# Lightning attention into a locality-gated expert layer: weights asked for behind the rows of x, routing's products sooner, first pair's preparation ahead of its gates, triples' turning later

## The chip, the cores and the metric

The kernel runs on one core of a Trainium2 chip. The metric is the device time of one execution, in microseconds (us). Before the change the median of three runs is 476.42 us (474.8 to 478.07).

The engines are named as in the profile: PE multiplies matrices (PEld is its weight load), DVE is the vector engine, ACT the scalar engine, POOL issues the gathers and scatters by index, SP issues most plain transfers. Each engine has one queue and works it off in order. An instruction that waits holds up everything behind it on its engine.

## The reference

Linear attention with a decay per head over 4 sequences of 768 positions (8 heads of 64), then an expert layer over the 3072 rows of 512:

```python
x = attention_out.transpose(0, 2, 1, 3).reshape(B, S, H * D)      # 4, 768, 512
logits = x @ w_gate                                               # 8 experts
local_gate = sigmoid(x @ w_local)
for b, s in order:
    fresh_e = argmax(logits[b, s])
    e = fresh_e if s == 0 or local_gate[b, s] < 0.5 else prev_e   # keep the expert of the row before
    prev_e = e
    p = softmax(logits[b, s])
    out[b, s] = p[e] * (relu(x[b, s] @ w1[e]) @ w2[e])            # w1: 512x1024, w2: 1024x512
```

All of it is float32, the matrix products too.

## The kernel before

**Attention, 0 to about 98 us.** 24 steps `s`, one for each chunk of 128 positions of each sequence, chunk by chunk. The finished rows are written to a DRAM tile `x_dram`, some by `rows_of` and some in groups by `turned_rows` and `group_out`. The last group is four transfers (L305) out of an `inp` tile of the pool `load`. Routing is worked out beside it in three parts of 8, 4 and 12 chunks (`fresh_experts`, `along_sequences`, `experts_of`, `ranks`, `masks`, `chances`), part 2 coming after the last step.

**First tiles and routing of part 2, about 98 to 163 us.** Three tiles (`KA = 3`) of 128 rows of one expert each are computed by plain products: `hidden` (first layer, halves of 4 blocks), `output` (second layer), `written` (gate and scatter). Their experts are 0, 1 and 2 where each expert has 128 rows in the first half of the chunks. Weights lie in two buffers `w1t[0..1]`, `w2t[0..1]`, and `weights(g)` loads an expert only if the buffer doesn't hold it. Once the attention's pools are closed a pool `act` takes their space. Its tiles `stay`, `run`, `tot` and the rest of routing's part 2 may not be written before what lay there has been read.

Part 2 of routing is a chain: `along_sequences(2)` (PE L438, DVE L441 and L447), `experts_of(2)` (PE L454, DVE L456), `ranks(2)` (PE L465 and L466, ACT L468, DVE L474 and L478), `other_tiles` and `tokens_to_other_tiles` (some 45 small DVE instructions), `brought(1, ...)` (DVE L678 fills `val`) and `masks(2)` (DVE L490), then `by_slots(1, ...)` (PE L688, DVE L697), which gives the rows that each later tile gathers. All of routing's products write one PSUM tile, `pr`, in different columns. `by_slots(0, (2, 3, 4))` gives the gates of the first three tiles in the same way. `moved` turns a gathered tile: 16 small ACT copies (L807) after a DVE `flipped` (L800).

**Pairs and triples, about 163 us to the end.** A unit is the rest of one expert: a pair (256 rows) or a triple (320). Each layer is done with 7 block products in place of 8, on sums of blocks of the weights (`sums_1`, `sums_2`, in place in the weight buffers) and of the rows (`sums_of_x`). With these inputs three pairs are followed by five triples, and three half tiles (`hooks_of_halves`) are worked in between the first two pairs' products. The functions `pair` and `triple` turn the next unit's rows (`unit_flipped`, `unit_moved`) between the present unit's products. A triple does its first layer in two halves of seven products each (L1061), then `second_layer` (L1066), with `steps(n)` between its products.

Between routing and the first pair stands a block whose order on PE, DVE, SP and ACT is written out by hand (it begins `unit_weights(0)`, and ends `written(last, i)`). In the block ahead of it the order on PE, DVE, SP and POOL is written out, and that on ACT is made by the scheduler. The orders are the text of the change. What decides is which instruction stands ahead of which on each engine.

Of the kernel before, what the change touches and what calls it, by code (L numbers as in the profile page):

```python
# [68 lines left out]
def kernel(  # L69
# [9 lines left out]
    nc = tc.nc  # L79
# [584 lines left out]
    def brought(i, ks):  # L664

        n, (g0, g1) = NT if i else NA, span(i)
        if 0 in ks:
            hit = nows["hit"] = pools[i].tile([P, n, g1 - g0], BF16, name=f"hit{i}", bufs=1)
            nc.vector.tensor_tensor(hit, whole[:, g0:g1].unsqueeze(1).broadcast_to([P, n, g1 - g0]),
                                    nows["to"].unsqueeze(2).broadcast_to([P, n, g1 - g0]), ALU.is_equal)  # L670
        hit = nows["hit"]
        if i:
            val = w1t[2].rearrange("p t f -> p (t f)").bitcast(BF16)[:, n * ks[0] * (g1 - g0):n * (ks[-1] + 1) * (g1 - g0)]
            val = nows["val"] = val.rearrange("p (n k g) -> p n k g", n=n, k=len(ks))
        else:
            val = nows["val"] = rt.tile([P, n, len(ks), g1 - g0], BF16, name=f"val{ks[0]}", bufs=1)
        for j, k in enumerate(ks):
            nc.vector.tensor_tensor(val[:, :, j], hit, parts[:, :n, k].unsqueeze(2).broadcast_to([P, n, g1 - g0]),  # L678
                                    ALU.mult)
# [118 lines left out]
    def flipped(xq, xg):  # L798

        nc.vector.transpose(xq, xg)  # L800
# [21 lines left out]
    def output(i, w, fs=range(FT)):  # L822
        for f in fs:
            nc.tensor.matmul(pys[i], lhsT=hq[f // 4, i][:, f % 4], rhs=w2t[w][:, f], start=(f == 0), stop=(f == FT - 1))  # L824
# [18 lines left out]
    def gate_of(g):  # L843
        i, j = at(g)
        return gate[i][:, j:j + 1]

    def written(g, i):
        nc.vector.tensor_scalar(yt[:, i], pys[i], gate_of(g), None, ALU.mult)
        scatter(g, yt[:, i])

    def number(k, n, engines=None):
# [14 lines left out]
    def extra_work(s, k):  # L866
        if (s, k) in extras:
            extras[s, k]()

    with tc.manual_schedule(engines={PE, DVE, SP, POOL}):  # L870
# [16 lines left out]
        for s in range(NS):  # L887
            if s + LOADS - 1 < NS:
                loaded(s + LOADS - 1)
            if s + 4 < NS and s != 1:  # L890
                prepare(s + 3)
            if s in QUARTERS:
                j = QUARTERS.index(s)
                nc.sync.dma_start(out=w1t[0][:, j], in_=w1_src(0)[:, j])
            if s == NS - 4:
                nc.sync.dma_start(out=w2t[0], in_=w2_src(0))
                weights(0)
            if s == NS - 1:
                nc.sync.dma_start(out=w1t[1], in_=w1_src(1))
                nc.sync.dma_start(out=w2t[1], in_=w2_src(1))  # L900
            if s + 1 < NS and s not in (1, 2, 3, 4, 5):
                scores(s + 1)
            if s + 1 == NS:
                first_turned()
            from_state(s)
            if s % B == 1 and s > B:
                logits(s // B - 1)
            if s == 5:
                scores(6)
            extra_work(s, 0)  # L910
            if s + 4 == NS:
                prepare(NS - 1)
            if s % B == 0 and s:
                gates(s // B - 1)
            mix(s)
            if s == 0:
                update(0)
                query_powers(0)
            if s in (1, 2, 3, 4):
                scores(s + 1)  # L920
            if s == 1:
                query_powers(1)
                prepare(4)
            if s:
                update(s)
            if s > 1 and s - 1 not in TURNED:
                rows_of(s - 1)
            for r in [r for r in TURNED if TURNED[r] == s]:
                turned_rows(r)
                if r + 1 not in TURNED or r % B == B - 1:  # L930
                    group_out(r // B)
            extra_work(s, 1)
        x_ctx.close()
        act = ctx.enter_context(tc.tile_pool(name="act", bufs=2))
        w1t.append(act.tile([P, DT, F], F32, name="w1_2", bufs=1))
# [49 lines left out]
        hidden(0, 0, 0, (2, 3))  # L985
        weights(1)
        moved(xtt[1], xq, (2, 3))
        logits(NC - 1)
        rows_of(NS - 1)
        fresh_experts(2)  # L990
        hidden(0, 0, 1, (0, 1, 2))
        flipped(xqs[1], xgt[0])
        along_sequences(2)
        by_slots(0, (2, 3, 4))
        hidden(0, 0, 1, (3,))
        moved(xtt[0], xqs[1])
        output(0, 0, (0,))
        experts_of(2)
        output(0, 0, (1, 2))
        ranks(2)  # L1000
        output(0, 0, range(3, FT))
        other_tiles()
        tokens_to_other_tiles()
        written(0, 0)
        weights(2)
        masks(2)
        brought(1, (0, 1))
        hiddens(1)
        output(1, 1, (0, 1))
        by_slots(1, (0, 1))  # L1010
        pair_ahead(0)
        other_owners()
        other_numbers()
        output(1, 1, range(2, FT))
        chances(2)
        written(1, 1)
        brought(1, (2, 3, 4))


    def a1(u, i, k):  # L1020
# [178 lines left out]
    def triple(u):  # L1199
# [9 lines left out]
        for half in range(2):  # L1209
            ms = range(2 * half, 2 * half + 2)  # L1210
            lo, hi = 2 * half, 2 * half + 2

            def active(f, i, c):
                relus(hq[f, i][:, lo:hi], c[:, :, :P], ACT.Relu)
                relus(h3[f][:, lo:hi, HP * i:HP * i + HP], c[:, :, P:], ACT.Relu)

            def product(to, a, b, new=False):
                product_1(to, a, b, new, ms)

            h00, h01, h10, h11 = (hq[f, i][:, lo:hi] for f in range(2) for i in range(2))  # L1220
            hn = [hs[:, n, lo:hi] for n in range(3)]
            c01, c10, c11 = (parts3[half][:, i] for i in range(3))
            a, b, c = (bank(n) for n in ("ps0", "ps1", "po0"))
            product(a, a1(u, 0, 0), b1(u, 0, 0), True)
            nc.scalar.copy(c01, a)
            if next and not half:
                unit_flipped(0)
                later_rows(u, (0,))
                unit_moved(u + 1, 0, (0,))
            product(b, s1[:, 1], xst[:, 1], True)  # L1230
            tt(c10, c01, b, ALU.add)  # L1231
            sums_2(u, (2 * half,))
            if next and half:
                unit_moved(u + 1, 2, (0,))
            product(c, a1(u, 1, 0), b1(u, 0, 1), True)
            product(b, s1[:, 0], xst[:, 0])
            tt(c11, c01, b, ALU.add)
            tt(c11, c11, c, ALU.add)  # L1238
            active(1, 1, c11)
            sums_2(u, (2 * half + 1,))  # L1240
            if next and not half:
                unit_moved(u + 1, 0, (1,))
            product(a, a1(u, 0, 1), b1(u, 1, 0))
            active(0, 0, a)
            if next and half:
                unit_moved(u + 1, 2, (1,))
            product(c, a1(u, 1, 1), xst[:, 2])
            tt(c10, c10, c, ALU.add)
            active(1, 0, c10)
            tt(hn[0], h10, h00, ALU.add)  # L1250
            product(b, s1[:, 2], b1(u, 1, 1))
            tt(hn[1], hn[0], h11, sub)
            tt(hn[2], h11, h10, sub)
            tt(c01, c01, b, ALU.add)
            active(0, 1, c01)
            if next and not half:
                unit_moved(u + 1, 0, (2, 3))
                unit_flipped(2)
                later_rows(u, (2,))
        later_weights(u, (1,))  # L1260

        def steps(n):
# [9 lines left out]
                scatter(tile_of(u, 2), y3)  # L1272
            if not next:
                return
            if n < 4:
                unit_moved(u + 1, 1, (n,))
            if n in (1, 2):
                unit_moved(u + 1, 2, (n + 1,))
            if n in (2, 3, 4):
                sums_1(u + 1, (n - 1,))  # L1280
            if n == 5:
# [105 lines left out]

    with tc.manual_schedule(engines={PE, DVE, SP, ACTE}):
        last, i = KA - 1, (KA - 1) % 2
        unit_weights(0)  # L1390
        hidden(i, i, 0)
        by_slots(1, (2, 3, 4))
        hidden(i, i, 1)
        arm = number(0, GENERAL + 1)
        half_weights(0)
        both_halves()
        rows_out(1)
        ahead_half(0)
        unit_flipped(0)
        unit_flipped(1)  # L1400
        unit_moved(0, 0)
        sums_1(0, (0, 1, 2))
        unit_moved(0, 1, copy=nc.vector.tensor_copy)
        sums_1(0, (3,))
        output(i, i)
        sums_of_x(0)
        pair_ahead(1)
        written(last, i)

# [102 lines left out]
```

## Time and profile before

| | us |
|---|---|
| median of three runs | 476.42 |
| lowest and highest | 474.8, 478.07 |
| the profiled execution's own time | 474.79 |
| span of its trace, first to last instruction | 473.1 |
| mean granted clock of TensorE in it | 0.973 |
| PE busy, PEld busy | 432.2, 352.0 |
| DVE, ACT, POOL busy | 299.9, 202.8, 114.5 |

Times within the trace count from its first instruction. A row of the timeline has the start, the length, the engine, the line of the kernel, the operation, what is written and read, and how many instructions were merged. What stands in brackets is the idle time ahead of it and what ended it. A table by windows gives busy time for each engine within a stretch and the clock that TensorE was granted there (1.00 is full speed). Line numbers are those of the kernel before.

### The profile page before, as it was taken

How to read it: one execution, taken by the hardware profiler on the slowest of the kernel's cores; microseconds unless marked ns; L12 is line 12 of the kernel's file. 1: busy time of each engine (PE TensorE's matmuls, PEld its weight loads, DVE VectorE, ACT ScalarE, POOL GpSimd, SP SyncE). 2: the span in 40 equal slices, each digit the busy share in tenths (PEclk: the TensorE clock that was granted, in tenths of full speed). 3: DMA queues.
4: the chain of work that ended last, by engine and by line, in shares of the span. 5: the costliest groups of instructions: out<-in, count | busy, mean ns of one | idle time of the engine just before them, and what ended most of it. 6: DMA issues, size and time to landing. Idle time of an engine off the chain costs nothing. (4 is left out here: it accounts for less than half of the span.)

```text
span 473.1 us, 9705 instructions
## 1 busy us (share of the span) xinstructions
PE 432.2 (91%) x3798; PEld 352.0 (74%) x3798; DVE 299.9 (63%) x595; ACT 202.8 (43%) x648; POOL 114.5 (24%) x119
## 2 busy tenths in 40 slices
PE   7999998883979979999999989998998998999992
PEld 7787777673567578878698976897697697779961
DVE  5687988852386778546378855757475475656610
ACT  4344565350410444353346568156536716632200
POOL 4576564400013120222031200221130030011001
PEclk9999999997899979999999999999999999999997
DMA  7999999977558989999367435164261533001001
GB/s 292 409 340 377 399 267 367 390 286 249 188 190 267 404 291 390 402 396 399 130 203 272 153 113 202 44 223 144 100 223 45 201 99 145 0 17 46 2 16 50
DMA packets 40343, 103.24 MB, mean 218 GB/s; under 512 B 2972, under 2 KB 10652, under 8 KB 38368
## 3 DMA queue, kind: packets, MB, share of 16 engines
q1 hardware_dynamic: 34784, 87.06, 50.3%
q0 software_dynamic: 4208, 13.37, 8.2%
q10 hardware_dynamic: 1296, 2.10, 1.2%
q8 instruction: 32, 0.52, 0.4%
q14 instruction: 23, 0.19, 0.1%
HBM read 98.33 MB, written 12.91 MB: 235 GB/s over the span
## 5 line engine op out<-in xcount | busy, mean ns | idle before, releaser
L1061 PE MATMUL ps<-w,s 128*128 128x192 f32 x240 | 44.9, 330 | 8.3 <-DVE w L1231 6.1
L807 ACT COPY w<-xlast 32x128 f32<-32x128 f32 x160 | 47.3, 295 | 6.0 <-DVE xlast L800 2.1
L1061 PEld LDWEIGHTS ps<-w,s 128*128 128x128 f32 x240 | 39.3, 190 | 11.3 <-DVE w L1231 7.2
L833 POOL DMA_INDIRECT out_dram<-y,sidx x17 | 18.2, 1071 | 93.4 <-DMA w<-in_w_dram 38.4
L786 POOL DMA_INDIRECT xg<-x_dram,gidx x19 | 22.3, 1173 | 57.1 <-DVE lg L800 33.1
L1268 PE MATMUL pr<-w,w 128*128 128x512 f32 x80 | 35.1, 592 | 0.0
L216 DVE TENSOR_TENSOR sm<-ps,mask 128x512 f32<-128x512 f32 x46 | 29.4, 681 | 7.5 <-PE ps L204 4.1
L181 POOL TENSOR_TENSOR qd<-inp,lamq 128x512 f32<-128x512 f32 x20 | 25.8, 1290 | 25.2 <-DMA inp<-in_qkv_dram 8.1
L1066 PE MATMUL pk<-s,hsum 128*128 128x256 f32 x128 | 30.4, 380 | 0.1
L1066 PE MATMUL pk<-w,h 128*128 128x256 f32 x128 | 30.5, 381 | 0.0
L1061 PE MATMUL po<-w,w 128*128 128x192 f32 x160 | 30.3, 333 | 0.0
L1061 PE MATMUL ps<-w,w 128*128 128x192 f32 x160 | 29.3, 326 | 0.0
L252 PE MATMUL po<-sm,inp 128*64 128x128 f32 x384 | 27.6, 280 | 1.4 <-DVE sm L216 0.7
L1268 PEld LDWEIGHTS pr<-w,w 128*128 128x128 f32 x80 | 15.2, 190 | 17.0 <-issue 15.8
L1061 PEld LDWEIGHTS po<-w,w 128*128 128x128 f32 x160 | 26.0, 190 | 2.3 <-DVE part L1238 1.2
L252 PEld LDWEIGHTS po<-sm,inp 128*64 128x64 f32 x384 | 21.0, 136 | 8.9 <-issue 5.6
L833 POOL DMA_INDIRECT out_dram<-w,sidx x5 | 7.9, 1588 | 80.0 <-DVE w L1271 80.0
L1061 PEld LDWEIGHTS ps<-w,w 128*128 128x128 f32 x160 | 26.7, 190 | 0.3
L1066 PEld LDWEIGHTS pk<-s,hsum 128*128 128x128 f32 x128 | 23.9, 190 | 3.6 <-DVE hsum L1172 0.5
L1066 PEld LDWEIGHTS pk<-w,h 128*128 128x128 f32 x128 | 23.8, 190 | 3.4 <-issue 0.6
L817 PEld LDWEIGHTS ps<-xt,w 128*128 128x128 f32 x192 | 23.1, 197 | 2.9 <-issue 2.3
L824 PE MATMUL pk<-w,h 128*128 128x512 f32 x48 | 24.7, 663 | 0.0
(334 smaller groups left out, 873.9 us busy)
## 6 DMA issues: line engine op xcount, KB each, us to landing
w<-in_w_dram SPq DMA_DIRECT2D x31, 2048.0 KB, 13.3
inp<-in_qkv_dram SPq DMA_DIRECT2D x15, 1024.0 KB, 10.8
inp<-in_qkv_dram SPq DMA_DIRECT2D x10, 512.0 KB, 7.7
x_dram<-w SPq DMA_DIRECT2D x12, 256.0 KB, 5.5
inp<-in_qkv_dram SPq DMA_DIRECT2D x4, 768.0 KB, 8.5
x_dram<-xn ACTq DMA_DIRECT2D x8, 256.0 KB, 6.4
w<-in_w_dram SPq DMA_DIRECT2D x4, 512.0 KB
x_dram<-inp SPq DMA_DIRECT2D x4, 192.0 KB, 6.9
```

Of the source, the lines that this page charges most:

```text
L181: nc.gpsimd.tensor_tensor(qd, x[:, 0].rearrange("p (a i) -> p a i", i=P), lamq, ALU.mult)
L216: nc.vector.tensor_tensor(sm[:, u], ps[u], mask[:, u], ALU.mult)
L252: nc.tensor.matmul(head(a, u), lhsT=vn[:, a, u], rhs=sm[:, u, a], start=(not c and a < 2), stop=True, skip_group_check=True)
L786: nc.gpsimd.indirect_dma_start(out=xg, out_offset=None, in_=x_dram[:n, :], in_offset=bass.IndirectOffsetOnAxis(ap=gidx[i][:, j:j + 1], axi ...
L807: copy((xt(k) if callable(xt) else xt)[QP * j:QP * j + QP, :, at(k):at(k) + QP], blocks[QP * k:QP * k + QP, :, j])
L817: nc.tensor.matmul(ph[:, j], lhsT=w1t[w][:, d, P * f:P * f + P], rhs=xtt[i][:, d], start=(d == 0), stop=(d == DT - 1))
L824: nc.tensor.matmul(pys[i], lhsT=hq[f // 4, i][:, f % 4], rhs=w2t[w][:, f], start=(f == 0), stop=(f == FT - 1))
L833: apart(nc.gpsimd.indirect_dma_start(out=out, out_offset=bass.IndirectOffsetOnAxis(ap=sidx[i][:, j:j + 1], axis=0), in_=y, in_offset=None, ...
L1061: nc.tensor.matmul(to[:, j], lhsT=a[:, k, P * m:P * m + P], rhs=b[:, k], start=(new and not j and not k), stop=(k == 1), skip_group_check= ...
L1066: nc.tensor.matmul(to, lhsT=a[:, f], rhs=b[:, f], start=(new and not f), stop=(f == FT // 2 - 1), skip_group_check=True)
L1268: nc.tensor.matmul(pr, lhsT=h3[f // 4][:, f % 4], rhs=w2t[w][:, f], start=(f == 0), stop=(f == FT - 1))
```

## The change

- The transfers of the second expert's weights (`w1t[1]`, `w2t[1]`) are issued after the loop over the steps, so after the last group of rows, no longer in its last step.
- `flipped(xqs[1], xgt[0])` is moved ahead of the last `logits`; `along_sequences(2)` and `experts_of(2)` are moved up between the blocks of `hidden(0, 0, 1, ...)`; `by_slots(0, (2, 3, 4))` is moved down behind `ranks(2)` and, on DVE, `other_tiles`.
- `written` multiplies by the gate on ACT (`nc.scalar.mul`), no longer on DVE.
- `val` of the later tiles is put into `hs`, no longer into `w1t[2]`; `masks(2)` comes behind `brought(1, (0, 1))`; `by_slots(1, (0, 1))` comes one block of `output(1, 1, ...)` earlier.
- The first pair's weights are asked for as those of expert 0 as soon as `hiddens(1)` and `output(1, 1, ...)` have read the buffers, and again by condition if its expert is another.
- In the written-out block the first pair's rows and sums (`unit_flipped`, `unit_moved`, `sums_1`) and `brought(1, (2, 3, 4))` are spread between `hidden`, `by_slots` and `output`.
- In `triple`, the four groups of copies of the next unit's first tile are spread over both halves; the third tile's flip goes from the end of the first half to the end of the second, and its copies into `steps`; the sum `c01` and its activation come ahead of the three sums `hn`.

```diff
         if i:
-            val = w1t[2].rearrange("p t f -> p (t f)").bitcast(BF16)[:, ...]
+            val = hs.rearrange("p n f i -> p (n f i)").bitcast(BF16)[:, ...]
...
     def written(g, i):
-        nc.vector.tensor_scalar(yt[:, i], pys[i], gate_of(g), None, ALU.mult)
+        nc.scalar.mul(yt[:, i], pys[i], gate_of(g))
         scatter(g, yt[:, i])
...
-            if s == NS - 1:
-                nc.sync.dma_start(out=w1t[1], in_=w1_src(1))
-                nc.sync.dma_start(out=w2t[1], in_=w2_src(1))
...
             extra_work(s, 1)
+        nc.sync.dma_start(out=w1t[1], in_=w1_src(1))
+        nc.sync.dma_start(out=w2t[1], in_=w2_src(1))
         x_ctx.close()
...
         moved(xtt[1], xq, (2, 3))
+        flipped(xqs[1], xgt[0])
         logits(NC - 1)
         rows_of(NS - 1)
         fresh_experts(2)
-        hidden(0, 0, 1, (0, 1, 2))
-        flipped(xqs[1], xgt[0])
+        hidden(0, 0, 1, (0,))
         along_sequences(2)
-        by_slots(0, (2, 3, 4))
+        hidden(0, 0, 1, (1, 2))
+        experts_of(2)
         hidden(0, 0, 1, (3,))
         moved(xtt[0], xqs[1])
-        output(0, 0, (0,))
-        experts_of(2)
-        output(0, 0, (1, 2))
         ranks(2)
+        output(0, 0, (0, 1, 2))
+        other_tiles()
+        by_slots(0, (2, 3, 4))
         output(0, 0, range(3, FT))
-        other_tiles()
         tokens_to_other_tiles()
         written(0, 0)
         weights(2)
+        brought(1, (0, 1))
         masks(2)
-        brought(1, (0, 1))
         hiddens(1)
-        output(1, 1, (0, 1))
+        nc.sync.dma_start(out=w1t[1], in_=w1_src(0))
+        output(1, 1, (0,))
         by_slots(1, (0, 1))
         pair_ahead(0)
         other_owners()
+        output(1, 1, range(1, FT))
+        nc.sync.dma_start(out=w2t[1], in_=w2_src(0))
         other_numbers()
-        output(1, 1, range(2, FT))
         chances(2)
         written(1, 1)
-        brought(1, (2, 3, 4))
...
# in triple(u), halves 0 and 1
             if next and half:
-                unit_moved(u + 1, 2, (0,))
+                unit_moved(u + 1, 0, (2,))
...
             if next and half:
-                unit_moved(u + 1, 2, (1,))
+                unit_moved(u + 1, 0, (3,))
...
             active(1, 0, c10)
+            if next and half:
+                unit_flipped(2)
+                later_rows(u, (2,))
+            product(b, s1[:, 2], b1(u, 1, 1))
+            tt(c01, c01, b, ALU.add)
+            active(0, 1, c01)
             tt(hn[0], h10, h00, ALU.add)
-            product(b, s1[:, 2], b1(u, 1, 1))
             tt(hn[1], hn[0], h11, sub)
             tt(hn[2], h11, h10, sub)
-            tt(c01, c01, b, ALU.add)
-            active(0, 1, c01)
-            if next and not half:
-                unit_moved(u + 1, 0, (2, 3))
-                unit_flipped(2)
-                later_rows(u, (2,))
...
# in triple's steps(n)
-            if n < 4:
+            if n == 0:
+                unit_moved(u + 1, 2, (0, 1))
+            if n == 1:
+                unit_moved(u + 1, 2, (2, 3))
+                unit_moved(u + 1, 1, (0, 1))
+            if n in (2, 3):
                 unit_moved(u + 1, 1, (n,))
-            if n in (1, 2):
-                unit_moved(u + 1, 2, (n + 1,))
...
# the block ahead of the first pair
-        unit_weights(0)
+        first = expert(1, 0)
+        nc.sync.dma_start(out=w1t[w_of(0)], in_=w1_src(first), cond=first != 0, cond_hint=False)
+        nc.sync.dma_start(out=w2t[w_of(0)], in_=w2_src(first), cond=first != 0, cond_hint=False)
+        half_weights(0)
+        unit_flipped(0)
+        unit_flipped(1)
+        brought(1, (2, 3, 4))
         hidden(i, i, 0)
+        sums_1(0, (0,))
+        unit_moved(0, 0)
         by_slots(1, (2, 3, 4))
+        ahead_half(0)
         hidden(i, i, 1)
-        arm = number(0, GENERAL + 1)
-        half_weights(0)
+        sums_1(0, (1, 2))
         both_halves()
         rows_out(1)
-        ahead_half(0)
-        unit_flipped(0)
-        unit_flipped(1)
-        unit_moved(0, 0)
-        sums_1(0, (0, 1, 2))
-        unit_moved(0, 1, copy=nc.vector.tensor_copy)
+        unit_moved(0, 1, (0, 1, 2))
+        arm = number(0, GENERAL + 1)
+        unit_moved(0, 1, (3,), copy=nc.vector.tensor_copy)
+        sums_of_x(0)
+        output(i, i)
         sums_1(0, (3,))
-        output(i, i)
-        sums_of_x(0)
         pair_ahead(1)
         written(last, i)
```

More of the change, by code (lines that the diff above doesn't have):

```diff
@@ L672, in brought @@
         if i:
-            val = w1t[2].rearrange("p t f -> p (t f)").bitcast(BF16)[:, n * ks[0] * (g1 - g0):n * (ks[-1] + 1) * (g1 - g0)]
+            val = hs.rearrange("p n f i -> p (n f i)").bitcast(BF16)[:, n * ks[0] * (g1 - g0):n * (ks[-1] + 1) * (g1 - g0)]
             val = nows["val"] = val.rearrange("p (n k g) -> p n k g", n=n, k=len(ks))
```

## The prediction

> **What bounds the kernel now.** I read the page's head, then the waits of PE, because PE is the engine that is nearly always busy.
>
> ```profile
> span 473.1 us, 9705 instructions
> PE 432.2 (91%) x3798; PEld 352.0 (74%) x3798; DVE 299.9 (63%) x595; ACT 202.8 (43%) x648; POOL 114.5 (24%) x119
> ```
>
> ```profile
> PE pr L688 <- DVE run L447: 8.1, 1, 8.1
> PE ps L1061 <- DVE w L1231: 6.1, 4, 1.5
> PE ps L1061 <- DVE xs L1042: 3.2, 1, 3.2
> PE pr L688 <- DVE w L678: 2.5, 1, 2.5
> PE ps L1061 <- DVE part L1254: 2.2, 5, 0.5
> ```
>
> Each row gives the sum, the count and the longest. PE's product of part 2 of routing waits once for 8.1 us, the triples wait 6.1 + 2.2 = 8.3 us, the first pair 3.2. The rest of the idle time is small pieces, and all else is PE's own work. So an edit is worth what it takes from these five waits. A second price hangs on them, which the table by windows shows (busy time of PE first, granted clock at PEclk):
>
> ```profile
> 119.45:122.86 3.41, 3.41 (x7) 0.99 (x6) 0.26 (x1) 3.19 (x11) 0.00 (x0) 0.50 0.74 210
> 136.51:139.93 3.42, 0.95 (x5) 0.40 (x4) 3.33 (x4) 0.00 (x0) 1.63 (x1) 1.00 0.22 85
> 139.93:143.34 3.41, 3.41 (x27) 2.28 (x27) 1.82 (x10) 0.00 (x0) 1.10 (x1) 0.50 0.00 0
> 279.87:283.28 3.41, 2.07 (x13) 2.07 (x14) 2.74 (x4) 1.77 (x6) 1.02 (x1) 1.00 0.12 20
> ```
>
> These are stretches between changes of the clock. A stretch with 0.95 us of PE work was followed by one at half clock, which cost half of its 3.41 us. One with 2.07 us busy was granted full speed, and so is all that follows in the triples. After 119.45 to 122.86, full but at half clock, the clock was up again (the next row is 1.00).
>
> **The change, part by part.** All times of the new order below are on the clock of the old trace.
>
> *Weights behind the rows.* SP issues the weights first, the rows wait behind them, and DVE waits for the rows:
>
> ```profile
> 99.11 0.46 SPq L900 DMA_DIRECT2D w<-in_w_dram  x1
> 100.16 9.62 SPq L305 DMA_DIRECT2D x_dram<-inp  x4
> ```
>
> ```profile
> 105.56 0.31 DVE L320 TENSOR_REDUCE lt<-pl 128x36 f32<-128x144 f32 x1 [4.83 <-PE pl L319]
> 107.15 0.70 DVE L800 STREAM_TRANSPOSE lg<-xg 128x512 f32<-128x512 f32 x1
> 115.25 0.55 DVE L441 TENSOR_SCALAR stay<-pr 4x384 bf16<-4x384 f32 x1 [7.40 <-DMA x_dram<-xlast]
> 115.83 1.00 DVE L447 TENSOR_TENSOR_SCAN run<-stay,carry,pr 4x384 bf16<-4x384 bf16 x1
> ```
>
> The row of L441 names the transfer of `xlast`, yet `stay` lies in the pool that takes the attention's space, and `xlast` does not. I read it as a wait for the four group transfers, whose issue alone took 9.62 us. What such transfers need otherwise:
>
> ```profile
> L305 SPq DMA_DIRECT2D x_dram<-w x12: 325/784/1851, 26.8 to 63.0; - x12
> DMA to landing us min/median/max: 3.8/5.8/7.5
> ```
>
> Four issues from 100.16 put the last at about 100.2 + 3 x 0.78 = 102.5, and it lands between 106.3 and 110.0, by the median at 108.3. The weights then go out at about 103.5. The four MB would be there by about 115, as now; the products that need them start at 122 below, so that costs nothing. If the rows landed as late as 110, 1.7 us would come back.
>
> *Routing's products sooner.* PE's rows:
>
> ```profile
> 105.72 2.84 PE L817 MATMUL ps<-xt,w 128*128 128x128 f32 x24
> 108.50 0.33 PE L438 MATMUL pr<-identb,each 128*4 128x128 bf16 x3
> 128.21 7.31 PE L817 MATMUL ps<-xt,w 128*128 128x128 f32 x64
> 155.49 7.11 PE L824 MATMUL pk<-w,h 128*128 128x512 f32 x16
> ```
>
> So a block of `hidden` (8 matmuls) is 0.93 us and a block of `output` (2 matmuls) 0.89. The flip of 0.70 now stands ahead of L320 on DVE. Its target shares the buffer `lg` with the logits that PE is reading, so I let it start where L320 did: marks at 107.85 in place of 107.15. PE does one block from 105.72, waits 1.2 us for the marks and runs L438 until 108.2. L441 and L447 run from 108.3 to 109.85. PE meanwhile does two blocks, so L454 is done at 110.15, the last block at 111.1, `ranks`' two products at 111.2. ACT's Relu of that block ends at 111.6 and its queue goes on with the copies:
>
> ```profile
> 119.85 5.07 ACT L807 COPY xt<-lg 32x128 f32<-32x128 f32 x16
> ```
>
> ```profile
> 125.22 0.38 DVE L474 TENSOR_TENSOR_SCAN incl<-go,tot 128x104 f32<-128x104 bf16 x1 [3.79 <-ACT tot L468]
> 134.87 0.17 DVE L627 TENSOR_TENSOR to<-to,late 128x12 f32<-128x12 f32 x1
> 135.62 1.75 DVE L490 TENSOR_TENSOR lane<-countb,place 128x1536 bf16<-128x1536 bf16 x1
> 138.20 1.68 DVE L678 TENSOR_TENSOR w<-hit,parts 128x696 bf16<-128x696 bf16 x2
> 141.28 0.22 DVE L697 COPY got<-pr 128x58 f32<-128x58 f32 x1 [1.41 <-PE pr L688]
> ```
>
> `ranks`' copy to `tot` stands behind those 16 copies now, and I leave it there: 111.6 + 5.1 + 0.25 = 116.95 for L474. From L474 to the end of L627 are 9.82 us, the gates' three small instructions are put in between (0.6), `hit` and `val` take 138.20 + 1.68 - 137.37 = 2.51, then `masks` 1.75: `val` at 129.9, the masks at 131.65. The multiplication by the gate leaves DVE. On ACT it waits for the gate until 124.4 and the Relus of `hiddens(1)` stand behind it, but these come later.
>
> *What is late next on PE.* `by_slots(0)` now writes `pr` behind `ranks`. Its columns are free, but if the tile is guarded as a whole, PE must wait for ACT's and DVE's reads of `pr` (L468, L478). The old trace cannot show it, the order being another. The bounds are no wait, with PE going on at 113.9, and a wait until 0.75 us after L474 starts, 117.7. I take the wait, as the first row of the waits shows this same product held by a read of `pr`. It leaves a gap of 3.8 us, after which I allow one and a half stretches at half clock, 2.5 us lost. From 118.1 PE has 5 blocks of `output` (4.45), `hiddens(1)` (7.31) and a block (0.89), with the clock 15.2: 133.3. That is past 131.65, so the 2.5 us wait for `val` is gone, and L697 runs at 134.0 in place of 141.28. With no wait at 113.9, PE would get to `by_slots(1)` at 127.0, idle there until the masks at 131.65, and have its slow stretch behind that. Both ways end within half a microsecond of each other.
>
> The Trainium skill, "TensorE: Matmul & The Clock Gate", section on why this matters for your kernels, says that gaps of up to about 3 us between bursts leave the clock up, and that a whole idle window (about 3.4 us) takes it down. The trace disagrees: 0.95 us of work in 3.42 was enough idleness to lose it. By the page's rule my 3.8 us gap may or may not hold a whole window, and without one PE would be at `by_slots(1)` 2.5 us sooner, of which the masks leave 1.6, inside the forecast's own range.
>
> *First pair.* From L697, PE still has 7 blocks of `output` (6.2 us): 140.2. `hidden` half 3.65, `by_slots` 1.0, half 3.65, `output` 7.11 and 0.49 of branching would start the pair at 156.1 if nothing waits. DVE's rows, ACT's and POOL's:
>
> ```profile
> 146.93 0.18 DVE L512 CAST parts<-room 128x12 bf16<-128x12 f32 x1
> 158.09 4.90 ACT L807 COPY xp<-xlast 32x128 f32<-32x128 f32 x16 [1.80 <-DVE xlast L800]
> 163.09 2.02 PE L1061 MATMUL ps<-xp,w 128*128 128x128 f32 x16 [0.49 <-issue]
> 174.68 1.95 PE L1061 MATMUL ps<-xs,s 128*128 128x128 f32 x16
> xg<-x_dram,gidx POOLq DMA_INDIRECT x19, 6.4
> ```
>
> From L697 to the end of `chances` are 147.1 - 141.3 = 5.8: 139.8. The gathers are issued at about 134.9 and 136.3; at 6.4 us to landing the second is there at 142.7, its flip done at 143.4, and three products of `val` (2.5) end at 145.9, where PE wanted them at 143.85. At best (no flip waits) they end at 143.6. I take half of the 2.0, so the pair starts at 157.1. ACT's 16 + 12 copies (4.90 + 3.7) with a Relu ahead and between run from 144 to 154, `sums_of_x` ends at 156, and the pair's second product wants it at 158.9: the 3.2 us wait is gone, and the slow stretch behind it. With the pair's first three products at 1.8 us, the fourth starts at 162.5 in place of 174.68. **The middle gives 12.2 us.**
>
> The early request for expert 0's weights is right if the first pair is expert 0's: from the reference's inputs it keeps 282 rows behind its first tile, not over 320, so it is, and the conditional loads are skipped. SP waits in them until w2 has landed, about 147.5. `half_weights(0)` stands behind and goes out at 152 now, so it is not later than before.
>
> *Triples.* What stalls in a triple, after its first half:
>
> ```profile
> 317.57 2.53 ACT L807 COPY w<-xlast 32x128 f32<-32x128 f32 x8
> 320.13 0.71 DVE L800 STREAM_TRANSPOSE xlast<-xgh 128x512 f32<-128x512 f32 x1 [3.24 <-ACT w L807]
> 316.34 0.55 DVE L1254 TENSOR_TENSOR part<-part,ps 128x384 f32<-128x384 f32 x1
> 326.92 0.43 DVE L1250 TENSOR_TENSOR hsum<-h,h 128x256 f32<-128x256 f32 x1 [0.63 <-ACT h L1214]
> 326.84 1.89 PE L1066 MATMUL pk<-w,h 128*128 128x256 f32 x8
> ```
>
> DVE's flip waits 3.24 us for ACT's copies out of the same buffer, and L1231 behind it holds a bank that PE wants; L1254, behind three sums, holds another. The change takes the flip out of that place and L1254 ahead of the sums, so both waits go: 8.3 us in all triples. The price is at the end of the second half: the flip (0.70) and L1254 (0.5) now stand ahead of `hsum`. With the second layer's start (326.84) as zero, the flip runs from -0.35, L1254 to 0.87, and the second `hsum` is ready at about 1.7, when PE wants it after its first product of 1.73. Below nothing there is nothing to gain; above, a Relu late by a group of four copies (2.53 / 2 = 1.27) would cost 1.2 in each of four triples. I take 0.1 each, by the arithmetic. The copies moved into `steps` are 32 in 10.1 us, under a second layer of 18.9. **The triples give 8.3 - 0.5 = 7.8.**
>
> **The sum**: 12.2 + 7.8 = 20.0 us, against the profiled execution's 474.79 (span 473.1 and 1.69 around it) 454.8. That execution lies 1.63 under the median of 476.42, so for a median I write 456.4.
>
> **Rivals.**
> - *The scheduler puts `tot` ahead of the 16 copies on ACT*, whose order is not written out there. Then DVE's chain is 5.1 us earlier, PE does not stop at `by_slots(0)` or `by_slots(1)`, and L697 follows at 127.7, 6.3 sooner: about 450. For it: the copies have no hurry. Against: now they go first. Chance 0.10.
> - *The wait stays*: `stay` waits for the second expert's weights too, or for the rows until 115. Then PE stands from 110 to 116.9 as now, L697 comes at about 140.9, the pair starts at 164.0 and its fourth product at 169.4, 5.3 us sooner: 476.4 - 5.3 - 7.8 = 463.3. For it: L441's row names a transfer that was issued after the weights. Against: their own issue precedes the rows', and DVE does not need them. Chance 0.17.
> - *The triples' wait moves to `hsum`*: 1.2 us in four of them leaves 7.8 - 4.4 = 3.4, so 460.8. Chance 0.08.
> - *Slower: the clock stays at half.* Place: PE from 117.7 to the first pair. If its new small gaps in each stretch kept the clock down, 35.5 us of work (0.4 + 4.45 + 7.31 + 0.89 + 0.66 + 6.2 + 3.65 + 1.0 + 3.65 + 7.11) would take 71, and the pair would start at 188.7, 25.6 late; the pair's own 6.2 and the triples' 7.8 come off: 11.6 slower, 488. It decides where no full stretch occurs at all; here `hiddens(1)` alone fills two. Chance 0.03.
>
> **How the numbers follow.** The forecast, 456.4, has 0.62; its own range is 452 to 460, from the bounds above (rows at 110, gathers at best or worst, the clock's 1.7 to 3.4). With the first three rivals the range is 449 to 467. About 1% (4.8 us) is what a measurement of this kernel can tell from no change. Faster by more 0.94, within 0.03 (the second and third rivals together with a late gather), slower 0.03.
>
> **What would show it.** PE's wait at L688 for `run` is gone, and L441 starts at about 108 to 110. If it still starts at 115, the second rival holds. L474 at 117 or 112 tells the first rival. A gap of some 4 us ahead of `by_slots(0)` tells the guard on `pr`. The pair's first product starts near 157 with no wait for `xs`. In triples the waits for L1231 and L1254 are gone; any wait for `hsum` at L1066 is the price. The prediction is wrong if the middle gives under 8 us.

## The result, and the profile after

After the change the median of four runs is 456.23 us (454.47 to 457.33), against 475.89 us (474.8 to 478.07) for four runs of the kernel before: a ratio of 0.9578, 95% interval 0.953 to 0.9625 (ratios here are of the means). The forecast was 456.4. The profiled execution took 454.47 us itself, of which its span is 452.7.

The page's row for the transfers of the rows of x (count, size of one, median us from issue to landing), and the waits of PE (sum, count and longest, in us):

```profile
x_dram<-inp SPq DMA_DIRECT2D x4, 192.0 KB, 3.5
```

```profile
PE pr L688 <- DVE where L478: 3.8, 1, 3.8
PE pr L688 <- DVE hsum L678: 3.7, 1, 3.7
```

The waits for `run` (8.1) and for `xs` (3.2), and both rows of the triples (6.1 and 2.2), are gone, and so is the one of 2.5 at `by_slots(1, (0, 1))`. In their place stand two waits at `by_slots`: 3.8 us for a read of `pr`, and 3.7 us for `val` (it lies in `hs` now, which the trace calls `hsum`).

What DVE did, from the marks to the last `by_slots`:

```profile
107.98 0.55 DVE L441 TENSOR_SCALAR stay<-pr 4x384 bf16<-4x384 f32 x1 [0.48 <-PE pr L438]
...
116.88 0.38 DVE L474 TENSOR_TENSOR_SCAN incl<-go,tot 128x104 f32<-128x104 bf16 x1 [6.56 <-ACT tot L468]
...
132.95 0.22 DVE L697 COPY got<-pr 128x58 f32<-128x58 f32 x1 [1.51 <-PE pr L688]
...
140.42 0.71 DVE L800 STREAM_TRANSPOSE xlast<-xg 128x512 f32<-128x512 f32 x1 [3.86 <-DMA xg<-x_dram,gidx]
141.06 0.13 DVE L506 TENSOR_SCALAR room<-room 128x12 f32<-128x12 f32 x1
...
145.36 0.88 DVE L678 TENSOR_TENSOR hsum<-hit,parts 128x696 bf16<-128x696 bf16 x1
```

`stay` starts 7.3 us sooner, `incl` (L474) 8.3, and L697 8.3. The flip at 140.42 waits 3.86 us for a gather, and the rest of `chances` (L506 and on) and `val` (L678) are behind it in DVE's queue. PE and its clock over the same time (in the table by windows: busy time of PE first, granted clock at PEclk):

```profile
117.67 0.46 PE L688 MATMUL pr<-val,lane 128*128 128x9 bf16 x12 [3.83 <-DVE where L478]
...
146.30 1.92 PE L688 MATMUL pr<-hsum,lane 128*128 128x87 bf16 x24 [3.72 <-DVE hsum L678]
...
159.18 1.95 PE L1061 MATMUL ps<-xp,w 128*128 128x128 f32 x16
...
164.53 0.72 PE L1061 MATMUL ps<-xs,s 128*128 128x128 f32 x5
```

```profile
114.95:118.37 3.42, 0.69 (x13) 0.59 (x14) 1.28 (x5) 1.81 (x7) 0.00 (x0) 1.00 0.52 197
118.37:121.78 3.41, 3.41 (x5) 1.33 (x4) 2.96 (x23) 0.00 (x0) 0.00 (x0) 0.50 0.46 118
...
142.26:145.67 3.41, 0.32 (x3) 0.14 (x3) 3.24 (x11) 2.90 (x10) 2.26 (x3) 1.00 0.98 320
145.67:149.09 3.42, 2.79 (x29) 2.79 (x29) 2.44 (x6) 2.30 (x8) 0.00 (x0) 0.50 0.97 371
```

The stretches in which the two waits lie had 0.69 and 0.32 us of PE work, and each was followed by one stretch at half clock. The pair starts 3.9 us sooner than before, its fourth product 10.15 sooner.

The triples, second of five: before, around the two waits and at the start of the third; then after, at its start, around the end of the first layer, and at the start of the third.

```profile
305.67 1.46 PE L1061 MATMUL ps<-w,w 128*128 128x192 f32 x8
...
314.98 1.46 PE L1061 MATMUL ps<-w,w 128*128 128x192 f32 x8
316.95 1.57 PE L1061 MATMUL ps<-w,s 128*128 128x192 f32 x8 [0.50 <-DVE part L1254]
318.35 1.46 PE L1061 MATMUL po<-w,w 128*128 128x192 f32 x8
321.33 1.57 PE L1061 MATMUL ps<-w,s 128*128 128x192 f32 x8 [1.52 <-DVE w L1231]
...
345.79 1.46 PE L1061 MATMUL ps<-w,w 128*128 128x192 f32 x8
```

```profile
293.14 1.46 PE L1061 MATMUL ps<-w,w 128*128 128x192 f32 x8
...
310.45 1.46 PE L1061 MATMUL ps<-w,s 128*128 128x192 f32 x8
311.75 1.89 PE L1066 MATMUL pk<-w,h 128*128 128x256 f32 x8
313.48 1.89 PE L1066 MATMUL pk<-s,hsum 128*128 128x256 f32 x8
...
330.70 1.46 PE L1061 MATMUL ps<-w,w 128*128 128x192 f32 x8
```

From start to start a triple took 345.79 - 305.67 = 40.12 us and takes 37.56. The first layer took 326.84 - 305.67 = 21.17 and takes 311.75 - 293.14 = 18.61: the whole 2.56 lies there. The second layer takes 18.95 in both, and no product of it waits for `hsum`.

**Where the 20.4 us of the span came from**: 10.15 up to the fourth product of the first pair (0.3 of it before routing's part 2: L319 runs at 104.48 on PE in place of 104.80), 10.2 between the starts of the first and the fifth triple (160.76 to 150.56), nothing elsewhere (the pairs lost 0.16, the last triple won 0.17).

### The profile page after: what moved, and what is told of

It reads as the page before. It is cut to its first block, busy times and chain, and to the rows that moved or that the text cites. A ratio compares the mean times of both kernels' runs of the same rounds, so it can differ in the third digit from the quotient of the medians.

```text
span 452.7 us, 9717 instructions
## 1 busy us (share of the span) xinstructions
PE 425.5 (94%) x3798; PEld 348.9 (77%) x3798; DVE 294.0 (65%) x580; ACT 208.7 (46%) x663; POOL 113.6 (25%) x119
## 5 line engine op out<-in xcount | busy, mean ns | idle before, releaser
L833 POOL DMA_INDIRECT out_dram<-y,sidx x17 | 17.2, 1010 | 86.9 <-DVE y L1120 29.7
L807 ACT COPY w<-lg 32x128 f32<-32x128 f32 x80 | 23.6, 295 | 1.9
```

The costliest lines, as they stand in the source:

```text
L807: copy((xt(k) if callable(xt) else xt)[QP * j:QP * j + QP, :, at(k):at(k) + QP], blocks[QP * k:QP * k + QP, :, j])
L833: apart(nc.gpsimd.indirect_dma_start(out=out, out_offset=bass.IndirectOffsetOnAxis(ap=sidx[i][:, j:j + 1], axis=0), in_=y, in_offset=None, ...
```

## The experiments

All ratios are to the kernel before, run beside the experiment on the same chip; spans and starts are of one profiled execution each. The attention does not take the same time in each trace: in the kernel after and in experiments 4 to 10 all that stands ahead of L441 is the same, yet it starts anywhere from 106.15 to 109.42 us. So a start in 4 to 10 is compared with that of the kernel after twice, as it stands and counted from L441.

**1. The weights' place alone.** Into the kernel before:

```diff
-            if s == NS - 1:
-                nc.sync.dma_start(out=w1t[1], in_=w1_src(1))
-                nc.sync.dma_start(out=w2t[1], in_=w2_src(1))
...
+        nc.sync.dma_start(out=w1t[1], in_=w1_src(1))
+        nc.sync.dma_start(out=w2t[1], in_=w2_src(1))
         x_ctx.close()
```

> The kernel before, with one edit: the second expert's weights are issued behind the last group of rows. If DVE's wait at L441 is for the rows, L441 starts at 108 to 110 in place of 115.25, PE's wait of 8.1 us at L688 shrinks to about 1.6, the slow stretch behind it goes, L697 of the later tiles comes about 7 us sooner, and the kernel is 6 to 8 us faster (near 469). Rival: the wait is for the transfer of xlast or for the weights themselves; then L441 stays at about 115 and the time does not change (within 1 us).

Measured: 468.33 us against 472.95, ratio 0.9873 (0.9795 to 0.9952); span 465.6, which is 7.5 less. By the ratio it is 6.0 us, within 2.3 to 9.7. Its DVE and its waits of PE:

```profile
108.48 0.55 DVE L441 TENSOR_SCALAR stay<-pr 4x384 bf16<-4x384 f32 x1 [1.07 <-PE pr L438]
```

```profile
PE pr L688 <- DVE w L678: 4.4, 1, 4.4
...
PE pr L688 <- DVE run L447: 1.7, 1, 1.7
```

`stay` no longer waits for any transfer. In the kernel before, the last of the four row transfers was issued at 108.3 and landed 6.9 us later, at 115.2, just ahead of `stay` at 115.25: what it waited for was the rows behind the weights. It was not the weights, which landed here at 112.9 and 118.2, behind `stay`, and not the transfer of `xlast`, which the row of before named: here it is issued only at 118.50. The releaser was named wrongly. The wait for `run` went from 8.1 to 1.7, and the one for `val` grew from 2.5 to 4.4: the other routing edits have their work from this.

**2. The triples alone.** The new body of `triple`, and nothing else, in the kernel before.

> The kernel before, with the new order inside triple alone. By the idle times that the waits show (8.3 us) less 0.5 for a new wait at the sums: 7.8 us faster. By the distance between the starts of the triples in the two traces (40.2 to 37.6 us in each of four, 0.5 in the last): 10.7 us faster, with no wait left in the triples. Rival: part of those 10.7 comes from the earlier stages' order, and alone the edit gives under 6.

Measured: 464.92 us, ratio 0.9822 (0.9754 to 0.9889); span 462.5, 10.6 less. No wait at L1231, L1254 or for `hsum` is left, and the wait for `run` stays, 8.4. The starts of the first and the fifth triple are 150.54 us apart, 160.76 before. So the part is worth what the starts of the triples say, not what the idle times say. The ratio, 8.4 us within 5.2 to 11.6, could not tell the two apart.

**3. The change with the weights ahead of the rows.** The reverse of the first diff, in the kernel after.

> The changed kernel, with the second expert's weights issued ahead of the rows again. If the rows are what L441 waits for, it starts at about 115 again and PE stands for 5 us or more ahead of experts_of; the middle loses 5 to 7 us (461 to 463). Rival: the new order alone, with more of PE's work ahead of the wait, hides it: within 2 us of the changed kernel.

Measured: 462.53 us, ratio 0.9783 (0.9736 to 0.9829); span 459.9, 7.2 more than after.

```profile
PE pr L454 <- DVE run L447: 8.2, 1, 8.2
```

The wait is back whole, at the product that now comes first. Against the triples alone all the changes of order before the first pair come to 464.92 - 462.53 = 2.4 us without the rows, and the first triple starts 2.4 sooner, but the two intervals overlap. By spans the three parts are 7.5 + 10.6 + (462.5 - 459.9) = 20.7, for 20.4 together; with one execution each, and intervals several us wide, that they fit so closely is partly luck.

**4. `by_slots(0)` in a free tile.** In the kernel after its products go to `pl`, so that no read of `pr` holds them:

```diff
-        pinv = pr[:, 2 * P:2 * P + len(ks) * w]
+        pinv = (pl if not i and 4 in ks else pr)[:, 2 * P:2 * P + len(ks) * w]
```

> The changed kernel, with the gates' product by_slots(0, (2, 3, 4)) written into another PSUM tile (pl) in place of pr. If the 3.8 us wait at it is the guard on pr, it goes. Theory: DVE's chain to the masks still ends at 131.4, PE only waits later at by_slots(1), by 4 to 4.5 us, and the time changes by less than 1 us. Rival: the wait costs what it shows, and the kernel is 3.5 to 5.5 us faster.

Measured: 454.44 us, ratio 0.9626 (0.9566 to 0.9687), span 450.5, 2.2 less than after, 0.5 of which lies ahead of L441.

```profile
PE pr L688 <- DVE hsum L678: 5.8, 2, 3.1
```

The 3.8 us wait was the guard on the tile, and it is gone. PE is at `by_slots(1)` some 6 us earlier and stands there for `val` (3.1) and the masks (1.2): L697 runs at 131.67 in place of 132.95, the pair starts at 157.08 in place of 159.18. Counted from L441 that is 0.7 and 1.6 us sooner. The interval of the time does not tell this kernel from after; the trace says that some 1.6 us came of it. One stretch at half clock follows the stand at `by_slots(1)`, and none follows the 2.7 us wait at the last `by_slots`, where the kernel after has its second.

**5. `ranks` ahead of the 16 copies.** In the kernel after, so that ACT's copy to `tot` precedes the turning:

```diff
-        moved(xtt[0], xqs[1])
         ranks(2)
+        moved(xtt[0], xqs[1])
```

> The changed kernel, with the text of ranks(2) ahead of moved(xtt[0], xqs[1]), so that ACT copies routing's totals before the 16 small copies of the turned tile. If those 16 copies (4.9 us) are what the routing chain waits for, L474 starts at 112 in place of 116.88, the wait of 3.8 us at by_slots(0) and the slow stretch behind it go, by_slots(1) is bound by PE, L697 of the later tiles comes at 127.5 in place of 132.95, and all behind moves with it: 5 to 6 us faster than the changed kernel (near 450). Rival: the copies only move their delay, since hidden of the third tile needs them; then under 2 us.

Measured: 451.79 us, ratio 0.9522 (0.9454 to 0.9589); span 448.1, 4.6 less than after. ACT's and DVE's rows:

```profile
111.18 0.23 ACT L468 COPY tot<-pr 128x96 f32<-128x96 f32 x1
111.30 4.89 ACT L807 COPY xt<-lg 32x128 f32<-32x128 f32 x16
```

```profile
111.45 0.37 DVE L474 TENSOR_TENSOR_SCAN incl<-go,tot 128x104 f32<-128x104 bf16 x1 [1.65 <-ACT tot L468]
```

```profile
PE pr L688 <- DVE hsum L678: 4.5, 1, 4.5
```

L474 starts 5.4 us sooner (4.9 from L441, which is the length of the copies), the guard holds nobody, L697 runs at 126.73, 6.2 sooner (5.7). The last `by_slots` stays held by the gathers, now 4.5 us, and two stretches at half clock in a row follow (139.36 to 146.19, the first with 1.96 us of work) where the kernel after has one. So the pair starts at 154.93, only 4.25 sooner (3.7). The time does not show the expected 5 to 6 us: by the two ratios it is 2.7, and the intervals overlap.

**6. `val` ahead of the flips.** In the kernel after:

```diff
+        brought(1, (2, 3, 4))
         unit_flipped(0)
         unit_flipped(1)
-        brought(1, (2, 3, 4))
```

> The changed kernel, with brought(1, (2, 3, 4)) ahead of the two flips in the block before the first pair. If the wait of 3.7 us at by_slots(1, (2, 3, 4)) comes of DVE standing in the flips for the gathers while the end of chances queues behind, val is ready at 141.4, PE goes on at 142.6 without a wait, the slow stretch from 145.7 goes too, the pair starts at 154.5 in place of 159.2 and the kernel is 4 to 5 us faster than the changed one. Rival: the rows turned later make the first pair wait for sums_of_x instead; then under 2 us, with a wait for xs at the pair's second product.

Measured: 457.55 us, ratio 0.9635 (0.9573 to 0.9697); span 454.4, 1.7 more than after. No wait at the last `by_slots` is left, so it was the flips that held `val`. The pair did start at 153.56, 5.6 sooner (5.1 from L441), and then:

```profile
PE pr L1306 <- DMA w<-in_w_dram: 4.5, 1, 4.5
```

```profile
150.93 0.09 SPq L1394 DMA_DIRECT2D w<-in_w_dram  x1
151.53 0.38 SPq L756 DMA_DIRECT2D w<-in_w_dram  x1
```

The row of the load that PE waited for (L756 again, issued at 172.2):

```profile
L756 SPq DMA_DIRECT2D w<-in_w_dram x1: 715/715/715, 172.2 to 172.2; - x1
...
  PE pr L1306: 4.5, 1
...
DMA to landing us min/median/max: 19.4/19.4/19.4
```

SP stood in the skipped conditional loads until the pair's w1 (L1393, at 141.26) and w2 (L1394) had landed, and asked for the first half tile's weights only at 151.53. PE did not wait for these: its first L1306, at 170.19, has no idle time ahead. It waited 4.46 us at its second, at 191.73, for the second half tile's w1, asked for at 172.21 behind five other loads of 2 MB from 151.53 on. That load took 19.4 us, and the 16 DMA engines show a busy share of 1.03 from 186 to 192 us. The two stretches from 190.20 to 197.03 were at half clock, with 1.88 and 3.42 us of work, which cost half of it, 2.6 us more. So the wait for `val` had covered these transfers.

**7. PE kept at work in the gap.** In the kernel after, 13 products of the identity, which nothing reads, ahead of `by_slots(1, (2, 3, 4))` (line numbers behind it are one to four higher):

```diff
+        fill = pg.tile([P, A, P], F32, name="po0")
+        for _ in range(FILL):
+            nc.tensor.matmul(fill[:, 0], lhsT=ident, rhs=ident, start=True, stop=True)
         by_slots(1, (2, 3, 4))
```

> The changed kernel, with 13 products of the identity into a free PSUM tile ahead of by_slots(1, (2, 3, 4)); their result is not used. They fill about 3 us of the 3.7 us wait for val and shorten nothing. If idleness takes the clock down, the stretch at half clock from 145.7 to 149.1 goes, and the pair starts 1.2 to 1.7 us sooner. Rival: the clock goes by the time since the last load, or by something else than PE's work; then the stretch stays and the pair starts no sooner.

Measured: 455.0 us, ratio 0.9585 (0.9521 to 0.9649), span 451.2, 1.5 less than after. The time cannot be told from after's; the clock can:

```profile
PE pr L689 <- DVE hsum L679: 0.8, 1, 0.8
```

```profile
144.91:148.33 3.42, 2.63 (x39) 2.46 (x37) 3.19 (x7) 2.64 (x9) 0.00 (x0) 1.00 0.98 360
148.33:151.74 3.41, 3.41 (x26) 2.87 (x26) 2.78 (x8) 0.93 (x3) 0.00 (x0) 1.00 0.22 85
```

The same late `val`, and no stretch at half clock: it is PE's idleness that costs the clock. The pair starts at 157.50, 1.7 us sooner, of which 1.3 are left from L441. Half of the 2.79 us of work in the slow stretch of the kernel after is 1.4.

**8. Numbers 5 and 6 together.**

> The changed kernel, with the edits of the two experiments before the fill together (totals ahead of the copies, val ahead of the flips). If both waits are independent, L697 comes at 127.5 and the pair starts at about 149.5, 9 to 10 us sooner: near 446. Rival: the gathers, issued at about 129 and landing 6.5 us later, hold the flips and the sums of x, and the pair's second product waits for xs by 1 to 4 us: 448 to 451.

Measured: 450.61 us, ratio 0.9502 (0.9429 to 0.9575); span 447.9.

```profile
PE pl L722 <- DVE few L706: 3.5, 1, 3.5
```

```profile
142.09 1.23 DVE L1039 TENSOR_TENSOR s<-w 128x1024 f32<-128x1024 f32 x1 [5.43 <-DMA w<-in_w_dram]
```

DVE stands at the first sum of the pair's weights until they land, with `got` and `few` behind it; PE also waits 1.4 us at the second half tile's L1306. The time falls into the rival's 448 to 451, but not by the rival's cause: no product waits for `xs`. The pair's w1 was asked for at 124.43 here, 6.5 us sooner than in number 6, and landed at 142.0, no sooner than there (141.2): the DMA engines' busy share was 1.03 from 124 to 142 us.

**9. Number 6 with `half_weights(0)` ahead of the two conditional loads.**

> The kernel after with brought(1, (2, 3, 4)) ahead of the two flips, as in e6, and in addition half_weights(0) ahead of the two conditional loads on SP. In e6 PE waited 4.5 us at L1306 for the half tile's weights, which SP issued only at 151.5, when w2 had landed. Theory (the gain of e6 went into that late issue): the half tile's weights go out at about 141, the wait at L1306 is gone and the slow stretch behind it (190 to 197, 3.4 us lost) too; the pair starts at 153.6 as in e6, and the time is 5 to 6 us under the kernel after, about 450. Rival (the weights as such come too late, the transfers being too many in this stretch): the conditional loads or the next unit's weights take over the wait, and the time stays at 455 to 458.

Measured: 453.41 us, ratio 0.9568 (0.9533 to 0.9604). L1306 waits no more: with the first half tile's 4 MB asked for early, the second half tile's w1 landed ahead of PE. But the time can't be told from after's 0.9578; the expected 5 to 6 us did not come; by the trace the pair starts 4.5 us sooner, 2.7 from L441.

```profile
PE pl L722 <- DVE few L706: 1.8, 1, 1.8
```

```profile
145.39 1.23 DVE L1039 TENSOR_TENSOR s<-w 128x1024 f32<-128x1024 f32 x1 [3.83 <-DMA w<-in_w_dram]
```

```profile
129.47 0.38 SPq L1008 DMA_DIRECT2D w<-in_w_dram  x1
133.55 0.37 SPq L756 DMA_DIRECT2D w<-in_w_dram  x1
...
137.68 7.27 SPq L758 DMA_DIRECT2D w<-in_w_dram  x1
145.30 0.08 SPq L1394 DMA_DIRECT2D w<-in_w_dram  x1
```

The row of L1008:

```profile
DMA to landing us min/median/max: 10.7/10.7/10.7
```

The pair's w1 was asked for at 129.47 (L1008) and landed 10.7 us later, at 140.1, hardly later than in number 6 (10.3 us). What came late was SP: the issue of the half tile's w2 (L758) took it 7.27 us, where the same took 0.38 in number 6, and the first conditional load (L1394, one line further on here) stands behind it. DVE's sum reads what that load could have written, and starts 0.09 us after SP has passed it, 5.2 us after w1 had landed; `got` and `few` stand behind. So the new order on SP took over the wait, not the transfer of w1.

**10. Number 8 with `half_weights(0)` early, and the first sum of weights behind the last `by_slots`.**

```diff
+        half_weights(0)
         nc.sync.dma_start(out=w1t[w_of(0)], ..., cond=first != 0, cond_hint=False)
         nc.sync.dma_start(out=w2t[w_of(0)], ..., cond=first != 0, cond_hint=False)
-        half_weights(0)
...
-        sums_1(0, (0,))
         unit_moved(0, 0)
         by_slots(1, (2, 3, 4))
         ahead_half(0)
+        sums_1(0, (0,))
```

> e8 (ranks ahead of moved, val ahead of the flips) with half_weights(0) ahead of the conditional loads, and with sums_1(0, (0,)) behind by_slots(1, (2, 3, 4)) and ahead_half(0). In e8 DVE stood 5.4 us at sums_1 for the first pair's w1 (landed about 142), which held got and few behind it, and PE 3.5 us at L722 for few, and had a slow stretch behind that. Theory: DVE passes to by_slots' copy at once, the waits at L722 (3.5) and L1306 (1.4) are gone with the slow stretch (1.7), and the first product of the pair still finds its sums ready: 5 to 6.5 us under e8, 444 to 446. Rival: the first pair's own weights bind then, PE waits at the pair's first products for sums_1 about as long as it waited at L722, and the time stays within 2 us of e8's 450.6.

Measured: 450.17 us, ratio 0.9482 (0.9456 to 0.9509). The rival's time held: the waits at L722 and L1306 are gone, the pair's first product starts at 149.79, and its second stands for sums that stand for the weights:

```profile
PE ps L1061 <- DVE xs L1042: 4.3, 1, 4.3
```

```profile
147.74 1.23 DVE L1039 TENSOR_TENSOR s<-w 128x1024 f32<-128x1024 f32 x1 [7.47 <-DMA w<-in_w_dram]
```

```profile
135.34 11.95 SPq L758 DMA_DIRECT2D w<-in_w_dram  x1
147.65 0.08 SPq L1394 DMA_DIRECT2D w<-in_w_dram  x1
```

Numbers 5, 8 and 10 overlap in their intervals, and the last has the lowest time. Its interval (to 0.9509) lies below that of the change (from 0.953), so it beats both kernels. Two things bound the middle there. The first pair's w1 landed 17.7 us after its issue at 127.13, so at 144.8, with the DMA engines' busy share at 1.03 from 124 to 154 us. And SP passed the first conditional load only at 147.65, for the same reason as in number 9, which holds DVE's sum another 2.9 us. An order with the half tile's w2 behind the conditional loads, or with fewer bytes ahead of w1, was not tried.

## Why the prediction was right or wrong

- **Weights behind the rows: right.** `stay` was put at 108.3 and started at 107.98; the four issues took 2.93 us in place of 9.62, and a group landed in 3.5 us in place of the 5.8 taken. The weights were there by 118.45 rather than 115, still ahead of their first product at 124.06. Experiments 1 and 3 show the part by itself from both sides. Experiment 3 is also the rival "the wait stays", which was priced at 463.3 and gave 462.53.
- **Routing's products: right in place, with the reason tested.** L474 was put at 116.95 and started at 116.88, behind the 16 copies. The rival with `tot` ahead was priced at 450 with L697 at 127.7; experiment 5 made it, and gave 451.79 and 126.73.
- **The guard on `pr`: right, and its price too low.** The gap of 3.8 us and its end at 117.7 came as written (3.83, 117.67). The statement that both ways end within half a microsecond of each other was not quite borne out: counted from L441, L697 is 0.7 sooner in experiment 4 and the pair 1.6. It set a slow stretch on both sides alike, which came so at `by_slots(0)` and `by_slots(1)`; that the free tile had one fewer further on lies in how its later wait fell into the clock's stretches.
- **L697 at 134.0: 132.95.** The clock's loss there was one stretch (1.7 us) where one and a half were allowed (2.5).
- **First pair: the step that failed.** The pair was put at 157.1 and started at 159.18. The flips were charged with half of a 2.0 us wait, and PE waited 3.72. The gathers landed as assumed: the second flip was put at 142.7 to 143.4 and ran at 141.86 to 142.57. But the step had all of `chances` ended at 139.8, ahead of the flips, with 2.5 us of `val` behind them. In the trace the flips stand inside `chances`: the first comes before L506, and after the second there were still its last instructions and `val`, up to 146.24, so 3.7 us in place of 2.5. In the kernel's text `chances(2)` is ahead of the flips; what put them inside it is not shown. PE, 1 us early, wanted it at 142.6. And no stretch at half clock was charged behind that wait: `by_slots` and the second half of `hidden` took 152.17 - 146.30 = 5.87 us in place of 4.65. The account of the 2.1 us: 1.05 gained at L697, 2.7 lost at the wait, 1.2 by the clock behind it, and 0.8 gained in blocks that were charged too long (7 blocks of `output` 5.89 for 6.2, the last `output` with the branching 7.01 for 7.60, a half of `hidden` 0.09 the other way). The middle gave 10.15 in place of 12.2.
- **`xs` and the half tile: right.** No wait for `xs`, and `half_weights(0)` went out at 151.9 (152 was written). That it was "not later than before" was true but thin: experiment 6 shows that the loads queued from there on, down to the second half tile's, were the next bound behind `val`. The expectation of experiment 9 named the first half tile's weights; the trace shows the second's.
- **Triples: right in mechanism, mis-sized.** 7.8 was forecast, 10.2 came, and no price at `hsum`. The term was taken from the idle times, 6.1 + 2.2. In the rows above the idle of one triple is 0.50 + 1.52 = 2.02, but from start to start it lost (316.95 - 314.98 - 1.30) + (321.33 - 318.35 - 1.30) = 2.35, and the first layer as a whole 2.56. The modelled end of a merged row (1.46 after its start) lies beyond the start of the next (1.30 after it), so the idle time is shown 0.16 short at each wait, and the row behind a wait takes 1.40 to the next in place of 1.30 (318.35 - 316.95), another 0.1.
- **The total** was met by luck: the two errors, 2.0 too much in the middle and 2.4 too little in the triples, cancelled. The range of 452 to 460 would have held either of them alone. A slip without effect: the terms of the slower rival add up to 35.3, not 35.5.
- **The clock.** The two gaps of 3.83 and 3.72 us took the clock down, and the one of 0.8 in experiment 7 did not; the gap of 2.47 in the kernel before took it down too (0.95 us of work in its stretch). The Trainium skill, "TensorE: Matmul & The Clock Gate", section on why this matters for your kernels, advises no gaps beyond about 3 us, and speaks of one idle window. The gap of 2.47 is shorter than that advice, and the stretches were not wholly idle: they had 0.95, 0.69 and 0.32 us of work. The slower rival, a clock that stays down, did not occur: in the kernel after it was up again after one stretch each time, with 3.41 and 2.79 us of work.

## What to carry to other kernels

Measure what a wait costs from start to start of the work around it, for the idle time that a profile shows can be short, and multiply by the repeats. When a wait at a busy engine is priced, look at every instruction between the waiting one and the one that matters in that queue, and charge the clock's stretch with it. And before a wait is removed, ask which transfer it was covering: here the second half tile's weights, and then the first pair's, took over as soon as the compute ahead of them was early. Read a landing from the transfer's own row, too: an instruction that starts late behind it can have stood for something else in the queue.

## What was not expected of the hardware

- Behind the attention, in all twelve traces, a stretch of 3.41 us with up to 1.34 us of matmul work (experiment 6, from 115.10) was followed by one at half clock, and one with 1.46 (experiment 4, from 141.33) or 1.52 (experiment 3, from 122.83) was not. One stretch does not fit: in the attention of experiment 6, from 80.97, 2.30 us of work were followed by half clock. What else counts there is open. At half clock, 2.79 us of work brought the clock back (the kernel after, from 145.67), and 2.67 did not (experiment 2, from 138.92).
- Taking 4 MB out from ahead of four transfers of 192 KB brought the landing from 6.9 us to 3.5 (one landing of the four is recorded in each trace), and the time of their issue from 9.62 to 2.93.
- An issue can hold the queue itself: L758 took SP 7.27 us in experiment 9 and 11.95 in experiment 10, with three or more loads of 2 MB not yet landed, and 0.38 in experiment 6 with one. What stands behind it on SP, a skipped conditional load too, waits meanwhile.
- With the DMA engines busy throughout, asking sooner did not land sooner: a load of 2 MB asked for at 124.43 landed at 142.0 (experiment 8), and asked for at 130.91 at 141.2 (experiment 6).
